# Gated attention and a state-space model, forward and backward: the last key block's transposes moved to TensorE, and the channel stage's constants to the head of the program

## The chip, the cores and the metric

The kernel runs on one core of one Trainium2 chip. The metric is the device time of one execution in microseconds. The time before is 2557.54 us, the median of three runs (2555.94 to 2568.38).

## The reference

The program computes an output and twelve gradients of one layer. The input x is 2048 tokens of 576 features. A gate mixes two branches:

```python
g = _sigmoid((x * gate_w).sum(-1, keepdims=True))
a = _A_ref(x, A_wqkv, A_wo)
b = _B_ref(x, B_A_re, B_A_im, B_B_re, B_B_im, B_C_re, B_C_im, B_log_dt, B_Dskip)
return g * a + (1 - g) * b
```

Branch a is attention with 32 heads of 18 features over all 2048 tokens, followed by the output projection. Branch b is a state-space model: for each of the 576 channels a kernel of length 2048 is made from 128 complex states, and convolved with the channel of x; a skip term is added. The reference returns this output and, by jax.vjp with a given grad_out, the gradients of x, of both attention weights, of the seven parameters of branch b that the convolution uses, of the skip and of the gate.

## The kernel before

The program has a projection stage, an attention stage, a channel stage for branch b, and a closing stage for the last gradients. The change touches the end of the attention stage and the start of the channel stage; this section keeps to those.

**Attention.** The heads are taken in 8 groups of 4, and the queries in 4 blocks of 512. A group with a query block is a unit, so there are 32 units. Each unit goes over 16 key tiles of 128 keys, in 32 steps of a loop whose counter is G; the backward work of a unit runs 39 steps (OFF) behind its forward work. When the forward work has run out, the last unit's backward work still goes on; that is the drain. The order on the engines is written out by hand (a manual schedule), so each engine does its instructions in the order of the code.

For one key tile, TensorE makes scores and dP in PSUM (`ps_P`), ScalarE makes the exponentials `eb` from them, and VectorE makes the products `ds` for four heads (L1488). From `ds` come three things: dV goes by `accV`, dQ by `accQ`, and dK by `accK`. dK needs `ds` turned, keys against queries, in a tile `dsT` that holds two key tiles. A burst of `accK` (`dk_half`) reads one or two of these tiles; there are four key blocks of four tiles, and the last one is tiles 12 to 15.

There are three ways to turn `ds`:

- a DMA transpose that SP issues (L1498), for the first heads of a tile;
- `turn` with `ds_tiles`: the fourth head (index 3), by eight TensorE transposes for a pair of tiles, into a PSUM tile `turn_p` and out again by one copy (L1121); `by_pe` says for how many tiles of a pair;
- `turn_mid`: in the last unit only, the heads 1 and 2 of a tile, by eight TensorE transposes into one of the two PSUM pairs that the scores use (`ps_turn`), and out by one copy (L1143).

So in the last unit head 0 comes by DMA, heads 1 and 2 by `turn_mid` and head 3 by `turn`. When the last unit's gradients are done, `store_grad` (L1086) issues DMA transposes of them on SP, and GpSimd copies these into `dtk` (L1091) and sends them off (L1092).

**The channel stage.** Its channels are taken in 18 blocks of 32. Its first lines (L1526 to L1537) make four constants: `pidx_i` (the partition's number, by GpSimd), `l0col` and `l1col` (the number, and the number plus one, by VectorE), and `sel` (a mask, by GpSimd). Then it opens block 0, in this order: `prep_rx` (VectorE and ScalarE copy x and its gradient to `RX`, L603 to L605; ScalarE's two scale by `l1col` and `l0col`), `load_en`, `wk_cast` (ScalarE, `wk`, L763), `k0` (64 small matmuls of `E1n` with `wk` into the PSUM tile `misc`), `k0_out` (ScalarE copies it to `K0c`, SP sends it to `Kp_d`, L780), `t0_load` (SP loads `T0w` from `Kp_d`, L864), `turn_e` (32 TensorE transposes of `E1n` into `etp`, L672, copied out to `E1e` by VectorE, L673), `m_sum` (eight small matmuls of `skw` with `sel` into `misc`), `m_fin` (ScalarE copies these to `RX` and `dDs_row`, L653 to L655), `m_skw` (SP loads `skw` of block 1, L642) and `uv` (32 matmuls `uvp` from `RX` and `E1e`, copied out by ScalarE, L709). After the opening the blocks follow one another, each with a long scan on VectorE.

Of the kernel before, what the change touches and what calls it, by code (L numbers as in the profile page):

```python
# [9 lines left out]
A = mybir.AluOpType  # L10
ACT = mybir.ActivationFunctionType
BF = mybir.dt.bfloat16
F32 = mybir.dt.float32
# [4 lines left out]
P = 128  # L18


def build(tc, aps, dbg_aps=None, stages=("s1", "attn", "post", "s4", "final")):
    nc = tc.nc
# [20 lines left out]
    NT = S // P  # L43
# [17 lines left out]
    with ExitStack() as gctx:  # L61
# [27 lines left out]
        SUB = 16  # L89
        NSUB = P // SUB  # L90
# [21 lines left out]
        DH2 = D // 2  # L112
        HALF = ((0, DH2), (DH2, D - DH2))
        W3 = 3 * H

        HB = P // 2
        assert D - (DC - 1) * P == HB
# [526 lines left out]
        def m_sum(b):  # L644
            skw = skws.pop(b)
            for v in range(CB // 8):
                mm(dkp(b)[:, v * 8:v * 8 + 8], lhsT=skw[:, v, :], rhs=Q["sel"])
# [113 lines left out]
        def wk_cast(b):  # L761
            wk = blk(b)["wk"] = Q["pw"].tile([P, 2, CB], BF, tag="wk", bufs=2, name="wk")
            nc.scalar.copy(wk, par_of(b)[:, 8:10, :])  # L763
# [187 lines left out]
        if "attn" in stages:  # L951
# [7 lines left out]
            with ExitStack() as ctx:  # L959
# [143 lines left out]
                def s_pair(kind):  # L1103
                    return apsp.tile([P, 2, KB], F32, tag="S", bufs=2, name="ps_" + kind)

                def by_pe(u, p):

                    return 2 if u == units[-1] else {1: 1, NPF: 0, NPF + 1: 1}.get(p, 2)

                def turn(tiles, outs):  # L1110

# [23 lines left out]
                def turn_mid(i):  # L1135

                    U = UN[units[-1]]
                    pt_ = s_pair("turn").rearrange("p a b -> p (a b)").bitcast(BF)[:, 0:2 * KB].rearrange("p (t b) -> p t b", b=P)
                    for x in range(2):
                        for qb in range(TPQ):  # L1140
                            nc.tensor.transpose(pt_[:, x * TPQ + qb, :], U["ds"][i][:, 1 + x, qb * P:(qb + 1) * P], ident_bf)
                    d_ = U["dsT", i // 2][:, i % 2, TPQ:3 * TPQ, :]
                    return lambda: (nc.scalar.copy if now[0] < NTOT + OFF else nc.vector.tensor_copy)(d_, pt_)  # L1143
# [218 lines left out]
                for G in range(NTOT + OFF + 24):  # L1362
# [37 lines left out]
                    if ("f1", G) in todo:  # L1400
                        acc = apsp.tile([P, KB], F32, tag="accO", name="accF")
                        evs.append(todo.pop(("f1", G))[0](acc))
                        e_done[0] += 1.4
                    elif G == NST + 5:
                        evs.append(turn(*do_tile(UN[units[0]])))
                    elif 0 <= m_ < NTOT // 8:
                        u_, kq = divmod(m_, NQ)
                        g, b = units[u_]
                        if slot in SLOTS:
                            nm, burst, h = SLOTS[slot]  # L1410
                            if h == 0:
                                acc = accB("acc" + nm)
                                fill(acc, NFILL[nm])
                                burst(g, b, kq, 0, acc)
                            else:
                                evs.append(burst(g, b, kq, 1, acc))
                                if nm == "Q" and kq == NQ - 1 and u_ < NU - 2:
                                    gq.append((UN[(g, b)], g, b))
                                elif nm == "Q" and kq == NQ - 1:
                                    at(("pre", G + 2), lambda g=g, b=b: store_grad(UN[(g, b)].pop("dqa"), g, (0,), b * TPQ))  # L1420
                                elif nm == "K" and b == NQ - 1:
                                    at(("pre", G + (2 if g == NG - 1 else (11, 13, 17, 17)[kq])), lambda g=g, kq=kq: store_grad(DKV.pop(("v", g, kq)).bitcast(BF), g, (2, 1), kq * TPQ, DKV.pop(("t", g, kq))))
                        else:
                            p = 2 * kq + (slot == 4)
                            t_, o_ = ds_tiles((g, b), p) if by_pe((g, b), p) else ([], [])
                            if p == 1 and gq:
                                t2, o2 = gb_tile()
                                t_, o_ = t2 + t_, o2 + o_
                            if G % NST == 5 and G // NST - 1 < NU:
                                t2, o2 = do_tile(UN[units[G // NST - 1]])  # L1430
                                t_, o_ = t2 + t_, o2 + o_
                            evs.append(turn(t_, o_))
                    if r2:
                        g, b, s2 = r2
                        T = grp_t[g]
# [38 lines left out]
                    for (kind, g, b, i, j, ps) in rows:  # L1474
                        U = UN[(g, b)]
                        if kind == "P1":
                            U["PT"][i, j // 2] = pt_tile()
                            nc.scalar.activation(U["PT"][i, j // 2], ps, ACT.Exp)  # L1478
                        elif kind == "P3":
                            e = eds.tile([P, 2, 448], BF, tag="eb", bufs=8, name="eb").rearrange("p a b -> p (a b)")  # L1480
                            U["eb"][(i[0], i[1], j)] = e[:, 0:KT]
                            U["eb"][(i[0], i[1], j + 2)] = e[:, KT:KW]
                            nc.scalar.activation(e, ps.rearrange("p x q -> p (x q)")[:, KB - KT:2 * KB], ACT.Exp)  # L1483
                        else:
                            if i not in U["ds"]:
                                U["ds"][i] = eds.tile([P, 4, KB], BF, tag="ds", bufs=5, name="ds")
                                U["dsn", i] = 0
                            nc.vector.tensor_tensor(U["ds"][i][:, j, :], ps, U["PT"][i, j // 2][:, j % 2, :], op=A.mult)  # L1488
                            U["dsn", i] += 1
                            while evs:  # L1490
                                evs.pop(0)()
                            nj = 1 if (g, b) == units[-1] else 3 if by_pe((g, b), i // 2) >= 2 - i % 2 else 4
                            if j == nj - 1:
                                p = i // 2
                                assert U["dsn", i] >= nj
                                if i % 2 == 0:
                                    U["dsT", p] = work.tile([P, 2, 4 * TPQ, P], BF, tag="dsT", bufs=3, name="dsT")
                                nc.sync.dma_start_transpose(out=U["dsT", p][:, i % 2, 0:nj * TPQ, :],  # L1498
                                                            in_=U["ds"][i][:, 0:nj, :].rearrange("p j q -> p (j q)"))
                    for e_ in mids + tail + todo.pop(("f2", G), []):  # L1500
                        e_()
                    while packs and packs[0][0] <= G:
# [8 lines left out]
        if "s4" in stages:  # L1511
# [6 lines left out]
            nc.vector.memset(ones_f, 1.0)  # L1518

            with ExitStack() as ctx:  # L1520
                pc = ctx.enter_context(tc.tile_pool(name="s4l", reuse_waits="tile", bufs=1))
                pw = Q["pw"] = Q["en", 2] = ctx.enter_context(tc.tile_pool(name="s4lw", reuse_waits="tile", bufs=1))
                ple_cm = tc.tile_pool(name="s4le", reuse_waits="tile", bufs=1)
                Q["ple"] = ple_cm.__enter__()
                pps = Q["ps"] = ctx.enter_context(tc.tile_pool(name="s4lps", reuse_waits="tile", bufs=1, space=bass.MemoryType.PSUM))
                pidx_i = pc.tile([P, 1], mybir.dt.int32, name="pidx_i")  # L1526
                nc.gpsimd.iota(pidx_i, pattern=[[0, 1]], base=0, channel_multiplier=1)
                l0col = pc.tile([P, 1], F32, name="l0col")
                nc.vector.tensor_copy(l0col, pidx_i)
                l1col = pc.tile([P, 1], F32, name="l1col")  # L1530
                nc.vector.tensor_scalar(l1col, l0col, 1.0, None, op0=A.add)
                sel = pc.tile([P, NSUB], F32, name="sel")
                nc.gpsimd.memset(sel, 1.0)
                nc.gpsimd.affine_select(out=sel, in_=sel, compare_op=A.is_ge, fill=0.0,
                                        base=0, pattern=[[-SUB, NSUB]], channel_multiplier=1)
                nc.gpsimd.affine_select(out=sel, in_=sel, compare_op=A.is_ge, fill=0.0,
                                        base=SUB - 1, pattern=[[SUB, NSUB]], channel_multiplier=-1)  # L1537
                Q["l0col"], Q["l1col"], Q["sel"] = l0col, l1col, sel
                Q["psM"] = lambda: pps.tile([P, 4, P], F32, tag="bk", bufs=4, name="psM")
                misc2 = Q["misc2"] = []  # L1540
# [7 lines left out]
                with tc.manual_schedule(engines={mybir.EngineType.SP}):  # L1548
                    prep_rx(0, dve_copy)
                    load_en(2, 0, nc.sync.dma_start)  # L1550
                    wk_cast(0)
                    k0(0)
                    k0_out(0)
                    t0_load(0)
                    turn_e(0, 0, 0, 4, dve_copy)
                    m_sum(0)
                    m_fin(0)
                    m_skw(1)
                    uv(0, 0)
                    prep_rx(1, dve_copy)  # L1560
# [406 lines left out]
```

## Time and profile before

| | |
|---|---|
| median of three runs | 2557.54 us |
| the profiled execution's own time | 2556.3 us |
| its span (first to last instruction) | 2554.6 us |
| mean granted clock of TensorE | 0.983 |
| busy TensorE, VectorE, ScalarE, GpSimd | 87%, 89%, 88%, 71% |
| the last accV burst of attention starts | 1969.19 us |
| the first uvp of the channel stage starts | 1992.57 us |

The profile is of one execution. PE is TensorE's matmuls, PEld its weight loads, DVE VectorE, ACT ScalarE, POOL GpSimd and SP SyncE, which issues DMAs. A row of the timeline has the start and the length in microseconds, the engine and line, the operation with output and inputs, and in square brackets how long the engine had been idle and what ended that. A row of the waits has the total, the number and the longest. In a table by stage the clock is TensorE's granted clock as a share of full speed.

### The profile page before, as it was taken

To read this page: it belongs to the slowest core of one execution; us is meant where nothing else is said; L and a number is where in the kernel's file an instruction comes from. 1 tells how busy PE (TensorE), PEld (TensorE's weight loads), DVE (VectorE), ACT (ScalarE), POOL (GpSimd) and SP (SyncE) were. 2 spreads that over 40 slices of the span, in tenths; PEclk is the share of its full clock that TensorE was granted. 3 is DMA by queue.
4 is the path that set the end of the run, shared out by engine and by line. 5 is a ranking of instruction groups with operands and counts; after the bars stand their busy time and mean duration, and the time that the engine had idled before them with its cause. 6 is when DMAs were issued, how large, how long until landed. Compare 5 with 4: busy or idle time off the path is not lost.

```text
span 2554.6 us, 72340 instructions
## 1 busy us (share of the span) xinstructions
PE 2232.1 (87%) x28463; PEld 1157.8 (45%) x28463; DVE 2275.6 (89%) x4121; ACT 2256.5 (88%) x2760; POOL 1822.1 (71%) x2829
## 2 busy tenths in 40 slices
PE   8988888888888888888888888888888899999989
PEld 4433333333333333333333333333333799999656
DVE  4849999999999989999999999999996799999964
ACT  5589999999999999999999999999987799998221
POOL 0389988888989888988888988898841255555331
PEclk9989999999999989999999999999999899999999
DMA  7759999999999999998999999999979789987996
GB/s 240 201 125 185 180 188 211 199 187 205 199 194 196 211 184 186 199 209 184 188 208 196 184 200 211 179 191 208 183 158 206 197 257 263 265 258 238 274 252 131
DMA packets 1272236, 519.05 MB, mean 203 GB/s; under 512 B 1187041, under 2 KB 1224530, under 8 KB 1269590
## 3 DMA queue, kind: packets, MB, share of 16 engines
q1 hardware_dynamic: 1223974, 368.17, 75.8%
q0 software_dynamic: 45904, 140.73, 20.5%
q10 hardware_dynamic: 2016, 5.51, 0.7%
q8 instruction: 223, 3.65, 0.6%
q14 instruction: 119, 0.97, 0.1%
HBM read 149.42 MB, written 96.94 MB: 96 GB/s over the span
## 4 chain that ended last, share of the span: by engine, by line
ACT 30%; PE 30%; DVE 21%; issue 4%; DMA 3%; POOL 0%; SPq 0%; DVEq 0%; ACTq 0%; POOLq 0%
ACT PT L1478 15%; ACT eb L1483 13%; PE ps_P L30 12%; DVE ds L1488 7%; PE accV L30 3%; DVE tz L734 3%; DVE wab L754 3%; DVE dvacc L1211 2%; PE accQ L30 2%; PE ps_dx L30 2%; PE accO L30 2%; DVE tz L737 2%; DVE HG L739 2%; DMA dsT<-ds 2%; PE accK L30 1%
## 5 line engine op out<-in xcount | busy, mean ns | idle before, releaser
L1488 DVE TENSOR_TENSOR ds<-ps_P,PT 128x512 bf16<-128x512 f32 x2048 | 1319.8, 683 | 62.7 <-PE ps_P L30 55.7
L1478 ACT ACTIVATE PT<-ps_P 128x1024 bf16<-128x1024 f32 x1024 | 1115.4, 1090 | 13.0 <-PE ps_P L30 11.1
L1483 ACT ACTIVATE eb<-ps_P 128x896 bf16<-128x896 f32 x1024 | 999.1, 976 | 21.3 <-PE ps_P L30 20.9
L30 PE MATMUL ps_P<-dOaT,VaT_g 32*128 32x512 bf16 x2048 | 784.6, 385 | 2.4 <-DVE ds L1488 1.4
L30 PE MATMUL ps_P<-QaT_g,KaT_g 32*128 32x512 bf16 x2048 | 403.2, 384 | 204.5 <-ACT PT L1478 173.6
L507 POOL TENSOR_TENSOR et<-eG,eT 128x448 f32<-128x448 f32 x576 | 542.4, 962 | 10.2
L30 PE MATMUL ps_P<-KaT_g,QaT_g 32*128 32x384 bf16 (+1 forms) x2048 | 401.0, 360 | 4.7 <-ACT eb L1483 0.8
L30 PEld LDWEIGHTS <-KaT_g 32*128 32x128 bf16 x2048 | 162.0, 91 | 492.4 <-issue 468.8
L507 POOL TENSOR_TENSOR Eo<-et,et 128x448 bf16<-128x448 f32 x288 | 327.1, 1136 | 20.3
L30 PEld LDWEIGHTS <-QaT_g 32*128 32x128 bf16 x2048 | 107.2, 91 | 239.0 <-issue 201.8
L30 PE MATMUL accO<-PT,Vtok_g 128*32 128x512 bf16 x2048 | 212.2, 392 | 0.5 <-DVE Ob L1059 0.5
L30 PE MATMUL accV<-eb,dOa 128*32 128x384 bf16 (+1 forms) x2048 | 183.0, 364 | 9.1 <-DVE dsT L1121 8.2
L30 PEld LDWEIGHTS <-VaT_g 32*128 32x128 bf16 x2048 | 184.6, 91 | 3.7 <-issue 2.1
L30 PE MATMUL accQ<-ds,Ktok_g 128*32 128x512 bf16 x2048 | 158.7, 386 | 24.7 <-DVE dvacc L1211 18.7
L30 PE MATMUL accK<-dsT,Qtok_g 128*32 128x256 bf16 x4096 | 159.7, 276 | 14.7 <-DMA dsT<-ds 12.4
L30 PEld LDWEIGHTS <-dOa 128*32 128x32 bf16 x3072 | 78.0, 95 | 122.2 <-issue 88.1
L1121 DVE COPY dsT<-turn_p 128x1024 bf16<-128x1024 bf16 (+1 forms) x216 | 130.5, 604 | 1.0 <-PE turn_p L1115 1.0
L673 ACT COPY E1e<-etp 128x1024 bf16<-128x1024 bf16 x132 | 125.3, 1065 | 3.1 <-PE etp L672 3.1
L1115 PE MATMUL turn_p<-ident_bf,ds 128*128 128x128 bf16 x1552 | 126.0, 221 | 2.1 <-DVE gb L1229 1.4
L30 PEld LDWEIGHTS <-Qtok_g 128*32 128x32 bf16 x4096 | 86.8, 96 | 82.1 <-issue 67.9
L507 POOL TENSOR_TENSOR et<-eT 128x32 f32<-128x32 f32 (+3 forms) x288 | 115.8, 422 | 11.4
L560 POOL DMA_DIRECT2D E_d<-Eo x144 | 84.7, 588 | 42.8 <-POOL Eo L507 42.8
(307 smaller groups left out, 3778.7 us busy)
## 6 DMA issues: line engine op xcount, KB each, us to landing
E_d<-Eo POOLq DMA_DIRECT2D x144, 256.0 KB, 3.8
E1n<-E_d POOLq DMA_DIRECT2D x30, 1024.0 KB, 7.5
T0w<-Kp_d SPq DMA_DIRECT2D x18, 1024.0 KB
xs<-xb_d POOLq DMA_DIRECT2D x28, 512.0 KB, 10.2
dsT<-ds SPq DMA_TRANSPOSE x512
dqkv_d<-dtk POOLq DMA_DIRECT2D x96, 72.0 KB, 4.4
Md_d<-mst SPq DMA_DIRECT2D x18, 288.0 KB
skw<-Md_d SPq DMA_DIRECT2D x72, 64.0 KB
```

Of the source, the lines that this page charges most:

```text
L30: return nc.tensor.matmul(out, lhsT=lhsT, rhs=rhs, start=start, stop=stop, **kw)
L507: nc.gpsimd.tensor_tensor(out, a, b, op=op)
L560: nc.gpsimd.dma_start(E_d[:, q // EQ, 0:EQ * 2 * P], Eo.pop(q).rearrange("p c r n -> p (c r n)"))
L673: copy(E_[:, 4 * q:4 * q + 4], pt_)
L734: nc.vector.tensor_tensor(tz[x], HG[:, :, k - 1].unsqueeze(1).to_broadcast([P, 2, 2, n, CB]), ZZ.unsqueeze(3).to_broadcast([P, 2, 2, n, CB ...
L737: nc.vector.tensor_tensor(tz[x][:, 0], tz[x][:, 0], UVk[:, :, :, k, :], op=A.add)
L754: nc.vector.tensor_tensor(wab, h_, w_, op=A.mult)
L1115: nc.tensor.transpose(pt_[:, x, qb, :], t_[:, qb * P:(qb + 1) * P], ident_bf)
L1121: (nc.scalar.copy if NTOT <= now[0] < NTOT + OFF else nc.vector.tensor_copy)(o_(), src_)
L1478: nc.scalar.activation(U["PT"][i, j // 2], ps, ACT.Exp)
L1483: nc.scalar.activation(e, ps.rearrange("p x q -> p (x q)")[:, KB - KT:2 * KB], ACT.Exp)
L1488: nc.vector.tensor_tensor(U["ds"][i][:, j, :], ps, U["PT"][i, j // 2][:, j % 2, :], op=A.mult)
```

## The change

The change has three parts.

The four constants are made at the head of the program, in the pool `const`, instead of at the start of the channel stage. All the tiles of the attention stage lie 128 bytes higher in SBUF by this; those of the channel stage stay where they were.

In the last unit, all four heads of the tiles 12 to 15 are turned by TensorE: `turn_mid` does sixteen transposes into a whole PSUM pair, and two copies take them out, ScalarE's for the heads 0 and 1 and VectorE's for the heads 2 and 3. In the built program VectorE's copy of a pair waits for ScalarE's. The DMA transposes of these four tiles are gone, and so are the two last rounds of `turn` (sixteen transposes, two copies) of this unit. TensorE's transposes are sixteen more in all.

In the opening of the channel stage `turn_e`, `m_sum` and `m_fin` of block 0 stand ahead of `k0`, `k0_out` and `t0_load`. The first matmul into `misc` for `k0` then comes behind the last copy of `m_fin`.

```diff
@@ setup
+        pidx_i = const.tile([P, 1], mybir.dt.int32, name="pidx_i")
+        nc.gpsimd.iota(pidx_i, pattern=[[0, 1]], base=0, channel_multiplier=1)
+        l0col = const.tile([P, 1], F32, name="l0col")
+        nc.vector.tensor_copy(l0col, pidx_i)
+        l1col = const.tile([P, 1], F32, name="l1col")
+        nc.vector.tensor_scalar(l1col, l0col, 1.0, None, op0=A.add)
+        sel = const.tile([P, NSUB], F32, name="sel")
+        nc.gpsimd.memset(sel, 1.0)
...
@@ by_pe
-                    return 2 if u == units[-1] else {1: 1, NPF: 0, NPF + 1: 1}.get(p, 2)
+                    if u == units[-1]:
+                        return 2 if p < NT // 2 - 2 else 0
+                    return {1: 1, NPF: 0, NPF + 1: 1}.get(p, 2)
@@ turn_mid
+                    if i >= NT - 4:
+                        for x in range(4):
+                            for qb in range(TPQ):
+                                nc.tensor.transpose(pt_[:, x * TPQ + qb, :], U["ds"][i][:, x, qb * P:(qb + 1) * P], ident_bf)
+
+                        def both():
+                            for y, copy in enumerate((nc.scalar.copy, nc.vector.tensor_copy)):
+                                sl = slice(2 * y * TPQ, 2 * (y + 1) * TPQ)
+                                copy(U["dsT", i // 2][:, i % 2, sl, :], pt_[:, sl])
+                        return both
@@ the loop over G
-                            evs.append(turn(t_, o_))
+                            if t_:
+                                evs.append(turn(t_, o_))
...
-                                nc.sync.dma_start_transpose(out=U["dsT", p][:, i % 2, 0:nj * TPQ, :],
-                                                            in_=U["ds"][i][:, 0:nj, :].rearrange("p j q -> p (j q)"))
+                                if (g, b) != units[-1] or i < NT - 4:
+                                    nc.sync.dma_start_transpose(out=U["dsT", p][:, i % 2, 0:nj * TPQ, :],
+                                                                in_=U["ds"][i][:, 0:nj, :].rearrange("p j q -> p (j q)"))
@@ the channel stage
-                pidx_i = pc.tile([P, 1], mybir.dt.int32, name="pidx_i")
-                nc.gpsimd.iota(pidx_i, pattern=[[0, 1]], base=0, channel_multiplier=1)
...
                     wk_cast(0)
+                    turn_e(0, 0, 0, 4, dve_copy)
+                    m_sum(0)
+                    m_fin(0)
                     k0(0)
                     k0_out(0)
                     t0_load(0)
-                    turn_e(0, 0, 0, 4, dve_copy)
-                    m_sum(0)
-                    m_fin(0)
                     m_skw(1)
```

VectorE at the end of the drain, before: from the last products of the tiles to `RX`, with the one copy of `turn_mid`, the one of `turn`, and the constants `l0col` and `l1col`.

```order
L1249 TENSOR_TENSOR dvacc<-dkacc,accK 128x512
L1488 TENSOR_TENSOR ds<-ps_P_38856,PT 128x512
L1488 TENSOR_TENSOR ds<-ps_P_38868,PT 128x512
L1488 TENSOR_TENSOR ds<-ps_P_38882,PT 128x512
L1488 TENSOR_TENSOR ds<-ps_P_38903,PT 128x512
L1488 TENSOR_TENSOR ds<-ps_P_38922,PT 128x512
L1211 TENSOR_TENSOR dvacc<-dvacc,accV 128x512
L1143 COPY dsT<-ps_turn 128x1024
L1229 SCALAR_TENSOR_TENSOR gb<-accQ,dqa 128x512
L1121 COPY dsT<-turn_p 128x2x512
L1518 MEMSET ones_f 128x1
L1529 CAST l0col<-pidx_i 128x1
```

The same place on VectorE in the changed program; `ds` is L1515 there, the pair's copy L1162.

```order
L1162 COPY dsT<-ps_turn 128x1024
L1515 TENSOR_TENSOR ds<-ps_P_38859,PT 128x512
L1275 TENSOR_TENSOR dvacc<-dkacc,accK 128x512
L1515 TENSOR_TENSOR ds<-ps_P_38881,PT 128x512
L1515 TENSOR_TENSOR ds<-ps_P_38893,PT 128x512
L1515 TENSOR_TENSOR ds<-ps_P_38898,PT 128x512
L1162 COPY dsT<-ps_turn 128x1024
L1515 TENSOR_TENSOR ds<-ps_P_38926,PT 128x512
L1515 TENSOR_TENSOR ds<-ps_P_38945,PT 128x512
L1237 TENSOR_TENSOR dvacc<-dvacc,accV 128x512
L1162 COPY dsT<-ps_turn 128x1024
L1255 SCALAR_TENSOR_TENSOR gb<-accQ,dqa 128x512
```

The copies of the tiles 13, 14 and 15 (and 12, above this piece) now stand among the products, and nothing stands behind `gb` but `ones_f` and the addition of `accK`.

ScalarE from the last `eb` of attention to the first `uv`, before:

```order
L1483 ACTIVATE eb<-ps_P_38918 128x896
L604 ACTIVATE RX<-RXn,l1col 128x32x15
L605 ACTIVATE RX<-RXn,l0col 128x32x15
L763 CAST wk<-par 128x64
L779 CAST K0c<-misc_39070 128x32
L653 CAST RX<-misc_39070 128x32
L654 ACTIVATE RX<-misc_39070,l0col 128x32
L655 CAST dDs_row<-misc_39070 1x32
L709 ACTIVATE UV<-uvp 128x64x8 x4
```

And in the changed program, where the copy of a pair is L1162 and the others have the numbers 13 higher:

```order
L1510 ACTIVATE eb<-ps_P_38941 128x896
L1162 COPY dsT<-ps_turn 128x1024
L617 ACTIVATE RX<-RXn,l1col 128x32x15
L618 ACTIVATE RX<-RXn,l0col 128x32x15
L776 CAST wk<-par 128x64
L666 CAST RX<-misc_39079 128x32
L667 ACTIVATE RX<-misc_39079,l0col 128x32
L668 CAST dDs_row<-misc_39079 1x32
L792 CAST K0c<-misc_39079 128x32
L722 ACTIVATE UV<-uvp 128x64x8 x4
```

ScalarE's last copy of attention is now that of tile 15, and `K0c` has moved from before the three copies of `m_fin` to behind them.

More of the change, by code (lines that the diff above doesn't have):

```diff
@@ L114, in build @@
         W3 = 3 * H
+        pidx_i = const.tile([P, 1], mybir.dt.int32, name="pidx_i")
[6 more added lines that the diff above has]
+        nc.gpsimd.memset(sel, 1.0)
+        nc.gpsimd.affine_select(out=sel, in_=sel, compare_op=A.is_ge, fill=0.0,
+                                base=0, pattern=[[-SUB, NSUB]], channel_multiplier=1)
+        nc.gpsimd.affine_select(out=sel, in_=sel, compare_op=A.is_ge, fill=0.0,
+                                base=SUB - 1, pattern=[[SUB, NSUB]], channel_multiplier=-1)
         HB = P // 2
@@ L1137, in turn_mid @@
                     U = UN[units[-1]]
-                    pt_ = s_pair("turn").rearrange("p a b -> p (a b)").bitcast(BF)[:, 0:2 * KB].rearrange("p (t b) -> p t b", b=P)
+                    pt_ = s_pair("turn").rearrange("p a b -> p (a b)").bitcast(BF).rearrange("p (t b) -> p t b", b=P)
+                    if i >= NT - 4:
[7 more added lines that the diff above has]
+                        return both
+                    pt_ = pt_[:, 0:2 * TPQ]
                     for x in range(2):
@@ L1520, in build @@
             with ExitStack() as ctx:
-                pc = ctx.enter_context(tc.tile_pool(name="s4l", reuse_waits="tile", bufs=1))
                 pw = Q["pw"] = Q["en", 2] = ctx.enter_context(tc.tile_pool(name="s4lw", reuse_waits="tile", bufs=1))
@@ L1525, in build @@
                 pps = Q["ps"] = ctx.enter_context(tc.tile_pool(name="s4lps", reuse_waits="tile", bufs=1, space=bass.MemoryType.PSUM))
-                pidx_i = pc.tile([P, 1], mybir.dt.int32, name="pidx_i")
-                nc.gpsimd.iota(pidx_i, pattern=[[0, 1]], base=0, channel_multiplier=1)
[L1528 to L1537, printed above, removed]
                 Q["l0col"], Q["l1col"], Q["sel"] = l0col, l1col, sel
```

## The prediction

> **What bounds the kernel now.** The page first: its span, the busy times of the engines, and the chain that ended last.
>
> ```profile
> span 2554.6 us, 72340 instructions
> PE 2232.1 (87%) x28463; PEld 1157.8 (45%) x28463; DVE 2275.6 (89%) x4121; ACT 2256.5 (88%) x2760; POOL 1822.1 (71%) x2829
> ACT 30%; PE 30%; DVE 21%; issue 4%; DMA 3%; POOL 0%; SPq 0%; DVEq 0%; ACTq 0%; POOLq 0%
> ```
>
> Three engines are near 88% busy and the chain passes among them; nothing the change does to busy time matters here (sixteen transposes more, two copies more). What can matter is a stretch in which all three stand still. The table by stage shows one, at the seam between attention and the channel stage (columns: length, busy PE, PEld, DVE, ACT, POOL, then the granted clock):
>
> ```profile
> 1955.00:1965.00 10.00, 9.26 (x113) 4.08 (x111) 8.67 (x15) 8.41 (x10) 0.84 (x2) 1.00 1.19 240
> 1970.00:1975.00 5.00, 1.80 (x27) 0.97 (x24) 2.33 (x4) 0.00 (x0) 0.00 (x0) 1.00 1.33 227
> 1975.00:1980.00 5.00, 0.95 (x24) 0.59 (x28) 0.06 (x1) 0.00 (x0) 0.00 (x0) 0.71 0.94 281
> 1980.00:1985.00 5.00, 0.87 (x17) 0.40 (x10) 1.69 (x4) 1.22 (x2) 3.28 (x7) 0.50 0.70 194
> 1985.00:1990.00 5.00, 3.89 (x85) 3.89 (x85) 1.15 (x3) 1.24 (x3) 3.46 (x8) 0.50 0.91 249
> ```
>
> From 1970 to 1985 TensorE works 3.6 of 15 us, VectorE 4.1, ScalarE 1.2. The waits around it say for what:
>
> ```profile
> ACT RX L604 <- DVE l1col L1531: 14.6, 1, 14.6
> PE accK L30 <- DMA dsT<-ds: 6.2, 2, 3.8
> PE misc L30 <- ACT wk L763: 5.2, 1, 5.2
> DVE l0col L1529 <- POOL sel L1533: 3.4, 1, 3.4
> ```
>
> TensorE waits twice for a DMA transpose of ds, 6.2 us. Then it waits 5.2 us for ScalarE's wk, which stands behind ScalarE's RX, which waits for l1col, which VectorE can't make before GpSimd's iota, which stands behind a GpSimd copy. The timeline puts these in order. TensorE:
>
> ```profile
> 1969.19 0.40 PE L30 MATMUL accV<-eb,dOa 128*32 128x384 bf16 x4 [0.65 <-ACT eb L1483]
> 1969.53 0.62 PE L1141 MATMUL ps_turn<-ident_bf,ds 128*128 128x128 bf16 x8
> 1972.22 0.61 PE L1115 MATMUL turn_p<-ident_bf,ds 128*128 128x128 bf16 x8 [0.79 <-DVE gb L1229]
> 1976.62 0.64 PE L30 MATMUL accK<-dsT,Qtok_g 128*32 128x256 bf16 x16 [3.80 <-DMA dsT<-ds]
> 1979.69 1.05 PE L30 MATMUL accK<-dsT,Qtok_g 128*32 128x256 bf16 x16 [2.43 <-DMA dsT<-ds]
> 1986.11 1.84 PE L30 MATMUL misc<-wk,E1n 128*128 128x1 bf16 x64 [5.24 <-ACT wk L763]
> 1987.82 3.33 PE L672 MATMUL etp<-ident_bf,E1n 128*128 128x128 bf16 x32
> 1990.98 1.01 PE L30 MATMUL misc<-sel,skw 128*128 128x8 f32 x8
> 1992.57 1.95 PE L30 MATMUL uvp<-RX,E1e 128*128 128x64 bf16 x32 [0.58 <-ACT dDs_row L655]
> ```
>
> The last accV burst of attention starts at 1969.19, accK ends at 1980.74, and uvp, the first real work of the channel stage, starts at 1992.57. So the seam has two pieces: 11.55 us from accV to accK's end, and 11.83 us from there to uvp. From uvp on, blocks follow one another by the three engines, and I found no wait there that ends at a fixed time, so a shift of uvp should reach the end of the program.
>
> **Part 1, the constants at the head.** GpSimd and VectorE at the seam:
>
> ```profile
> 1981.26 0.43 POOL L1091 COPY dtk<-dkacc 128x288 bf16<-128x288 bf16 x1 [14.43 <-DMA dkacc<-dvacc]
> 1983.27 0.15 DVE L1529 CAST l0col<-pidx_i 128x1 f32<-128x1 int32 x1 [3.44 <-POOL sel L1533]
> 1983.78 1.14 ACT L604 ACTIVATE RX<-RXn,l1col 128x480 bf16<-128x480 bf16 x1 [14.63 <-DVE l1col L1531]
> 1984.83 1.10 ACT L605 ACTIVATE RX<-RXn,l0col 128x480 bf16<-128x480 bf16 x1
> 1985.83 0.23 ACT L763 CAST wk<-par 128x64 bf16<-128x64 f32 x1
> ```
>
> With the constants in place, ScalarE runs RX and wk directly behind its last copy of attention, at about 1975 to 1977.4 (1.14 + 1.10 + 0.23), during TensorE's last accK. The wait of 5.2 us for wk goes to nothing. At the head of the program the five GpSimd instructions come in among others that nobody waits for:
>
> ```profile
> 0.80 0.20 POOL L66 MEMSET ident_bf<- 128x128 bf16 x1 [0.29 <-POOLq L1951]
> 5.42 0.69 DVE L232 COPY xT<-tr 128x1024 bf16<-128x1024 bf16 x1 [4.42 <-PE tr L229]
> 40.14 0.68 POOL L429 DMA_DIRECT2D QKV_d<-stg  x1 [36.56 <-ACT qn L408]
> ```
>
> GpSimd idles 36.56 us there and VectorE 4.42 us; cost nothing. If that cover were gone it would be about 1 us (five instructions at the 0.20 of ident_bf's row).
>
> **Part 2, transposes by TensorE alone.** Four DMA transposes leave SP, so the 6.2 us of waits for them end. In exchange each of key tiles 12 to 15 has sixteen transposes and a ScalarE copy with a VectorE copy behind it. What these last, and how far VectorE has room:
>
> ```profile
> 1967.30 1.02 ACT L1143 COPY dsT<-ps_turn 128x1024 bf16<-128x1024 bf16 x1
> 1962.69 0.69 DVE L1488 TENSOR_TENSOR ds<-ps_P,PT 128x512 bf16<-128x512 f32 x1 [0.55 <-PE ps_P L30]
> 1968.24 0.69 DVE L1488 TENSOR_TENSOR ds<-ps_P,PT 128x512 bf16<-128x512 f32 x1 [0.66 <-PE ps_P L30]
> 1970.26 0.69 DVE L1143 COPY dsT<-ps_turn 128x1024 bf16<-128x1024 bf16 x1
> 1971.47 0.69 DVE L1229 SCALAR_TENSOR_TENSOR gb<-accQ,dqa 128x512 bf16<-128x512 f32 x1 [0.53 <-PE accQ L30]
> ```
>
> This is the added wait. In the built program VectorE's copy of a pair waits for ScalarE's of that pair, and the ds products of the next tiles are queued behind it on VectorE; TensorE's ps_P banks, and ScalarE's eb behind them, wait for those. I estimate a hold of 0.75 us for each (1.0 us of copy less what VectorE still has to do of ds) and 0.69 us of copy, for tiles 12 to 14: 4.3 us of VectorE time in a drain that has idle time of 1.6 us there (the 0.55 and 0.66 above are the larger pieces). Propagated by hand, instruction by instruction, with these durations, the last accV comes 3.3 us later; bounds 0 (all in idle time) and 4.3 (none of it).
>
> Behind accV: 0.34 to tile 15's transposes, 1.2 for sixteen (two rows of eight, 0.62), ScalarE's copy 1.0, VectorE's 0.7, gb 0.6, then accK in two bursts of 0.6 (the row with 0.64): 5.0 us, where before it was 11.55 (accQ's sixteen matmuls now lie beside the copies). The first piece gains 11.55 − 5.0 − 3.3 = **3.2 us**, bounds 2.2 and 6.5.
>
> **Part 3, the opening's new order.** E1n's transposes (etp), m_sum and m_fin move ahead of k0. Of these only k0 needs wk, and the first uvp needs all. So from accK's end: etp, m_sum, a wait for m_fin on ScalarE, k0, uvp. The price of 32 etp at the full clock is half of this later row:
>
> ```profile
> 2000.03 3.82 PE L672 MATMUL etp<-ident_bf,E1n 128*128 128x128 bf16 x64
> ```
>
> 1.9 + 1.0 + 0.6 + 1.8 = 5.3 us, instead of 11.83: **6.5 us**. At 0.50, as granted before, etp is 3.3 and the rest alike: 6.7 us, gain 5.1. I take the full clock, because the longest idle of TensorE should now be about 1.5 us (accQ to accK) instead of 3.8, 2.4 and 5.2, and rows at 1970 to 1975 with 1.80 of 5 us busy still show 1.00. VectorE has meanwhile accK's addition, its part of RX (about 1 us, as ScalarE's) and four E1e copies at the 0.69 of its dsT copy: from 1977.6 these end at about 1982.1, uvp starts at 1982.9. That is the next thing to be late, by 0.8 us of room.
>
> [...]
>
> Moved on the queues: Kp_d, T0w and block 1's skw stand behind K0c on SP.
>
> ```profile
> 1988.20 0.32 SPq L780 DMA_DIRECT2D Kp_d<-K0c  x1
> 1993.54 0.32 SPq L864 DMA_DIRECT2D T0w<-Kp_d  x1
> 1993.95 2.54 SPq L642 DMA_DIRECT2D skw<-Md_d  x4
> 2003.69 1.01 PE L30 MATMUL misc<-sel,skw 128*128 128x8 f32 x8
> 2023.49 2.10 PE L30 MATMUL yp<-RX,T0w 128*128 128x32 bf16 x32
> ```
>
> K0c came 4.4 us before uvp and now comes with it, so these start some 4.8 us later against the rest. T0w has 30 us until yp; cost nothing. skw was issued until 1996.5 and used at 2003.69; it would be issued until about 1991.5 and be used at 1994.0. [...] I take 0; bound 2.
>
> **The sum.** 3.2 + 6.5 = 9.7 us. The profiled execution took 2556.3 us, 1.7 beyond its span, and becomes 2546.6; the median of three, 2557.54, lies 1.2 higher and would be 2547.8. I say **2547.2**. Bounds: 2.2 + 5.1 − 2 = 5.3 and 6.5 + 6.5 = 13.0.
>
> **Rivals.** The forecast: chance 0.61 for a gain of 5 to 12.
>
> A, the drain isn't stretched: VectorE's held copies fit into its idle time. The gain is 13.0, 2543.9; for it speaks that VectorE idles 1.6 us there, that one ScalarE copy (turn_p, 1.0 us) is gone, and that SP is freed; against it, VectorE at 8.67 of 10 us. [...] Chance of over 12.8: 0.13.
>
> B, VectorE's hold cascades: each late ds makes eb late and each late eb the next copy, twice the 4.3 us. The first piece then loses 2.1, and 6.5 − 2.1 leaves 4.4: 2552.5. Decided if the last accV comes more than 6.5 us later. Chance 0.13.
>
> C, the constants weren't the last thing that RX waited for: its memory comes free only with the DMA of dkacc, for which GpSimd at 1981.26 had waited 14.43 us. That DMA comes 3.3 later with the drain, so RX starts at 1984.6, wk is done at 1987.1, m_fin behind it at 1987.7, k0 at 1989.5, and uvp gains 3.1: 2553.8. For it: GpSimd's row. Against: in the new order RX waits only for ds, accQ and eb. It decides if RX starts after 1978.0, 2.5 us ahead of the end of m_sum. Chance 0.08.
>
> D, slower: the transposes take one of the two PSUM pairs that the scores also use, and keep it until VectorE's copy is through. If that copy comes behind all four ds products of a tile, the pair is held for 1.2 of transposes, 2.8 of ds (four of 0.69), 1.0 of ScalarE's copy and 0.7 of its own, 5.7 us, and if the next scores wait all that time, tiles 12 to 14 cost 17 us against the 13.0 that can be gained at most: 2561. It decides from 4.3 us a tile on. For it: two pairs alone; against: the scores have the other one, and ScalarE has no more copies than before. Chance 0.05, of which 0.02 over 0.5%.
>
> **The numbers.** A measurement of this kernel can tell about 0.5%, 12.8 us. Faster by more than that: A, 0.13. Slower: 0.02. Same: 0.85, with the forecast, B, C and most of D in it. The range leaves out about 2 in 10: from A's time less 2 us for the spread of the runs before, 2541.9, to C's 2553.8 and 1.7 more, 2555.5.
>
> **What would show it.** Right: accK without a DMA wait and its end near 1977.6; RX on ScalarE by 1976; etp directly behind accK at a clock near 1.00; uvp near 1982.9; later rows 9 to 10 us earlier. Wrong: a wait on ScalarE's RX for anything later than 1976; VectorE waits of over 2 us for ScalarE's dsT copies; uvp waiting for E1e; m_sum of block 1 waiting for skw; or later blocks that aren't earlier by what uvp is.

## The result and the profile after

The changed kernel takes 2592.15 us (2587.29 to 2600.18, six runs) where the kernel before takes 2557.47 in the same job: a ratio of 1.0128, with a 95% interval of 1.0111 to 1.0144. Forecast were 2547.2 us and no more than 2555.5. So the change costs 33 us by this ratio (35 by the medians) where 10 were to be gained.

The seam is not where they went. TensorE's rows there, in the changed kernel (they answer to those from 1969.19 to 1992.57 of before):

```profile
2013.95 0.62 PE L30 MATMUL accV<-eb,dOa 128*32 128x384 bf16 x4 [0.36 <-ACT eb L1510]
2014.50 1.89 PE L1157 MATMUL ps_turn<-ident_bf,ds 128*128 128x128 bf16 x16
2018.86 1.06 PE L30 MATMUL accK<-dsT,Qtok_g 128*32 128x256 bf16 x32 [0.80 <-DVE ones_f L1546]
2019.85 1.96 PE L685 MATMUL etp<-ident_bf,E1n 128*128 128x128 bf16 x32
2021.65 1.01 PE L30 MATMUL misc<-sel,skw 128*128 128x8 f32 x8
2023.24 0.17 PE L30 MATMUL misc<-dsk_row,ident_bf 1*128 1x32 bf16 x1 [0.58 <-ACT dDs_row L668]
2023.35 1.78 PE L30 MATMUL misc<-wk,E1n 128*128 128x1 bf16 x64
2024.99 3.38 PE L30 MATMUL uvp<-RX,E1e 128*128 128x64 bf16 x32
```

accK's two waits for a DMA are gone, and so is the wait for wk. (accV works on eb, as its row shows, and not on ds as the section on the kernel has it.) From accV to accK's end it is 5.97 us (forecast 5.0, before 11.55), from there to uvp 5.07 (forecast 5.3, before 11.83). But all of this lies some 40 us late. VectorE copies oT once in each of the 32 forward units, so the start of this copy in each unit shows when the delay came about. Before, units 1, 5, 6 and 32:

```profile
167.12 0.68 DVE L1047 COPY oT<-accO 128x512 f32<-128x512 f32 x1
387.56 0.68 DVE L1047 COPY oT<-accO 128x512 f32<-128x512 f32 x1
443.09 0.68 DVE L1047 COPY oT<-accO 128x512 f32<-128x512 f32 x1
1897.60 0.68 DVE L1047 COPY oT<-accO 128x512 f32<-128x512 f32 x1
```

The same four in the changed kernel:

```profile
169.81 0.68 DVE L1060 COPY oT<-accO 128x512 f32<-128x512 f32 x1
390.42 0.68 DVE L1060 COPY oT<-accO 128x512 f32<-128x512 f32 x1
452.00 0.68 DVE L1060 COPY oT<-accO 128x512 f32<-128x512 f32 x1
1937.48 0.68 DVE L1060 COPY oT<-accO 128x512 f32<-128x512 f32 x1
```

The delay is 2.7 us at unit 1, 2.9 at unit 5, 8.9 at unit 6 and 39.9 at unit 32. It grows in steps of 2.8 to 8.4 us at the units 6, 10, 14, 18, 22, 26 and 30, each the second of a group of heads (and by 2.3 at unit 7), and little or nothing in the units between, where at times a part is won back. None of the change's instructions stands there. What the engines wait for in unit 6 is seen on TensorE, VectorE and ScalarE:

```profile
427.90 1.04 PE L30 MATMUL accK<-dsT,Qtok_g 128*32 128x256 bf16 x16 [4.52 <-DMA dsT<-ds]
429.00 0.69 DVE L1269 COPY dkacc<-accK 128x512 f32<-128x512 f32 x1 [4.79 <-PE accK L30]
429.52 0.92 ACT L1510 ACTIVATE eb<-ps_P 128x896 bf16<-128x896 f32 x1 [4.86 <-PE ps_P L30]
```

A DMA transpose of ds lands 4.5 us too late for accK, and everything stands behind it. The waits of the whole attention stage (us 160 to 1895) and the hardware DMA queue in us 200 to 1900 (packets, MB, time that the packets took as a share of 16 engines), before:

```profile
PE accK L30 <- DMA dsT<-ds: 6.2, 6, 1.3
q1 hardware_dynamic: 1073798, 273.62, 91.8%
```

and in the changed kernel:

```profile
PE accK L30 <- DMA dsT<-ds: 31.8, 18, 4.5
q1 hardware_dynamic: 1052659, 268.32, 97.4%
```

accK's waits for dsT are 25.6 us longer there, where the delay grows by 37.2 (39.9 − 2.7); the rest was not traced. There are fewer packets in the window, as the program is slower, but they take more of the queue's time: 0.918 × 16 × 1700 us / 1073798 = 23.3 ns for one before, and by the same working 25.2 ns now. The queue carries the same transfers in the same order; what differs about them is where their tiles lie: 128 bytes higher, as the section on the change says.

### The profile page after: what moved, and what is told of

Read it like the earlier page. It is cut to its first block, busy times and chain, and to the rows that moved or that the text cites. A ratio compares the mean times of both kernels' runs of the same rounds, so it can differ in the third digit from the quotient of the medians.

```text
span 2585.6 us, 72360 instructions
## 1 busy us (share of the span) xinstructions
PE 2257.6 (87%) x28479; PEld 1163.5 (45%) x28479; DVE 2279.4 (88%) x4123; ACT 2260.4 (87%) x2760; POOL 1825.6 (71%) x2829
## 5 line engine op out<-in xcount | busy, mean ns | idle before, releaser
L1515 DVE TENSOR_TENSOR ds<-ps_P,PT 128x512 bf16<-128x512 f32 x2048 | 1321.1, 684 | 66.5 <-PE ps_P L30 57.1
L30 PE MATMUL ps_P<-QaT_g,KaT_g 32*128 32x512 bf16 x2048 | 408.4, 388 | 197.5 <-ACT PT L1505 168.3
```

The costliest lines, as they stand in the source:

```text
L30: return nc.tensor.matmul(out, lhsT=lhsT, rhs=rhs, start=start, stop=stop, **kw)
```

## The experiments

In the expectations below, e1 is the first kernel, e2 the second, and so on. What is said of a single place in a kernel is read from one profiled execution.

**The place alone, and the change without it.** Theory P: the 128 bytes cost the time. Theory H: something else in the change does, at the head or by way of the queues. The first kernel is the kernel before with nothing but a pad:

```diff
+        eds.tile([P, 32], F32, name="pad")
         d_aT = [eds.tile([P, 4, 512], BF, tag="ds", bufs=5, name="ds") for _ in range(DC)]
```

> The kernel before with nothing changed but an unused pad of 128 bytes ahead of attention's first tile, so that every attention tile lies where the changed kernel has it, and the channel stage's where they were. Theory P (place): the new addresses make the packets of the DMA queue longer, 25.2 instead of 23.3 ns each, and that alone costs the 39 us: 2557.5 + 39 = 2596, between 2588 and 2600, with the accK waits for dsT near 32 us. Theory H (the instructions at the head, or the drain's new transposes, through the queues): addresses don't matter, 2557.5 within 3.

Measured: ratio 1.0207 to before (1.0183 to 1.0231), 2615.16 us. That is more than the changed kernel, which has the seam's gain against it, and 15 us above the range forecast. The accK waits are 31.5 us, as forecast, and the packets take 25.2 ns:

```profile
q1 hardware_dynamic: 1040820, 265.55, 96.3%
```

The pad alone makes the kernel slower than the whole change does. The second kernel is the changed one with more padding at the same place:

```diff
+        eds.tile([P, 96], F32, name="pad")
         d_aT = [eds.tile([P, 4, 512], BF, tag="ds", bufs=5, name="ds") for _ in range(DC)]
```

> The changed kernel with a pad of 384 bytes ahead of attention's first tile: its tiles lie 512 bytes above those of before instead of 128. Theory P, if what counts repeats every 512 bytes or less: attention as before, and the seam's gain is left, some 7 to 8 us: 2549 to 2551. Theory H: 2590 as the changed kernel.

Measured: ratio 0.9973 (0.9961 to 0.9985), 2553.64 us where the kernel before takes 2560.99 in the same job. The gain of 7.4 us is as forecast, the time itself is above the range. In the third, the lines that make the constants stand at the channel stage again:

```diff
-        pidx_i = const.tile([P, 1], mybir.dt.int32, name="pidx_i")
...
+                pidx_i = pc.tile([P, 1], mybir.dt.int32, name="pidx_i")
```

> The changed kernel with the four constants made at the channel stage again, so that attention's tiles lie where they lay before; the transposes by TensorE and the new order of the opening stay. Theory P: no 39 us, and of the seam's gain what the wait for l1col leaves: drain 1 us, and RX at about the place it had, so that wk still comes late but etp and m_sum are done meanwhile: 4 to 6 us faster, 2551 to 2554. Theory H by the head: the same. Theory H by the drain's transposes: 2590.

Measured: ratio 0.9977 (0.9962 to 0.9993), 2556.62 us: 4.4 less than before, where 4 to 6 were forecast; the time itself is again above the range. The fourth has a pad of 128 bytes in the changed kernel:

```diff
+        eds.tile([P, 32], F32, name="pad")
         d_aT = [eds.tile([P, 4, 512], BF, tag="ds", bufs=5, name="ds") for _ in range(DC)]
```

> The changed kernel with a pad of 128 bytes: attention's tiles lie 256 bytes above those of before. Theory P with a period of 256 bytes (ds on a multiple of 256 again): 2549 to 2551. Theory P with a period of 512: anything from 2550 to 2600, since dsT then starts at another place in its 512 bytes. Theory H: 2590.

Measured: ratio 0.9964 (0.9949 to 0.9979), 2551.37 us, 9.6 less than before. The packets take 23.2 ns:

```profile
q1 hardware_dynamic: 1072879, 273.48, 91.6%
```

Theory H is out: with the same instructions and 256 or 512 bytes instead of 128, the change is a gain of about 0.3 to 0.4%. The third and the fourth also price the early constants at the seam: from accK's end to uvp it is 7.94 us in the third and 5.04 in the fourth, 2.9 less.

**Which tile.** ds starts on a multiple of 256 in the kernel before; dsT starts 96 above one. The fifth kernel moves ds by 128 and the rest by 256, the sixth moves all but ds by 128, both from the kernel before:

```diff
+        eds.tile([P, 32], F32, name="pad")
         d_aT = [eds.tile([P, 4, 512], BF, tag="ds", bufs=5, name="ds") for _ in range(DC)]
+        eds.tile([P, 32], F32, name="pad2")
         eb_t = [eds.tile([P, 2, 448], BF, tag="eb", bufs=8, name="eb") for _ in range(DC + 3)]
```

(the sixth without the first of the two pads)

> The kernel before with two unused pads of 128 bytes, one ahead of the ds tiles and one behind them: ds alone starts 128 bytes off a multiple of 256, and the rest of attention lies 256 bytes higher, where e4 showed no loss. Theory S (the source: the DMA transposes read ds in pieces that now cross a boundary at each multiple of 256): as slow as e1, 2595 to 2620, packets at 25 ns. Theory D (the destinations, dsT and PTt, or another tile): as before, 2555 to 2562, packets at 23.3 ns.

> The kernel before with one pad of 128 bytes behind the ds tiles: ds stays, everything else in attention lies 128 bytes higher. Theory S: 2555 to 2562. Theory D: 2595 to 2620. If both matter, both e5 and e6 are slower than before, by less than e1.

Measured: ratio 1.0184 (1.0155 to 1.0213), 2604.85 us, with ds moved, and 1.0027 (1.0006 to 1.0049), 2566.13 us, with the rest moved; the kernel before takes 2559.24 in this job. The fifth lies in theory S's range, the sixth 4 us above it. The queues' lines, the fifth first:

```profile
q1 hardware_dynamic: 1048196, 267.20, 96.3%
```

```profile
q1 hardware_dynamic: 1073732, 273.60, 91.6%
```

25.0 ns a packet against 23.2. It is the place of ds, the source of the transposes. What the rest adds is at most half a per cent, and not by the packets.

The eighth kernel asks for another distance, a pad of 64 bytes in the kernel before (`[P, 16]` instead of `[P, 32]`):

> The kernel before with a pad of 64 bytes ahead of attention's first tile. Theory S: any place off a multiple of 256 makes the 256-byte reads cross, so as slow as e1, 2595 to 2620. If instead 64 bytes cost less than 128 (2560 to 2590), the price goes by how a piece is cut, not by whether.

Measured: ratio 1.0186 (1.0152 to 1.0220), 2604.55 us, 25.1 ns, in the range of theory S. 64 bytes cost as 128 do.

**The destinations, and a second source.** In the seventh, on top of the fourth, the tile ahead of dOaT is 160 bytes longer, which brings dOaT, PTt, dsT, dvacc and gb to multiples of 256; the ninth brings 24 of the 41 PT buffers there too, which are sources of the PTt transposes.

```diff
-                        st["oT"] = work.tile([P, KB], F32, tag="oT", bufs=1, name="oT")
+                        st["oT"] = work.tile([P, KB + 40], F32, tag="oT", bufs=1, name="oT")[:, 0:KB]
...
-                        gT = work.tile([P, TPQ, 4, HP], BF, tag="gT", bufs=1, name="gT")
+                        gT = work.tile([P, KB + 32], BF, tag="gT", bufs=1, name="gT")[:, 0:KB].rearrange("p (t a b) -> p t a b", a=4, b=HP)
```

(the last two lines in the ninth alone)

> The changed kernel as in e4 (256 bytes up), and 160 bytes more ahead of dOaT, so that the destinations dsT and PTt and the sources dvacc and gb start on multiples of 256 instead of 96 above one. Theory S: the packets stay at 22.9 ns, 2551 within 3 (dvacc's few transposes alone may gain a little). Theory D: packets under 22.5 ns and faster than e4.

> As e7, with 64 bytes more behind attention's last work tile, so that 24 of the 41 PT buffers start on multiples of 256 instead of 192 above one. PT is the source of the 128 PTt transposes. Theory S holds for every source: packets about 0.2 ns shorter than e7's 23.20, and up to 4 us faster than e7's 2545. If the queue has room now, the packets shorten and the time stays.

Measured: ratio 0.9951 (0.9925 to 0.9977), 2545.24 us, for the seventh, and 0.9961 (0.9938 to 0.9984), 2549.88 us, for the ninth; both have packets at 23.2 ns, as the fourth has (the forecast for the seventh had it at 22.9). The intervals overlap, so neither the destinations nor PT can be told from nothing. The seventh came out 3 us below theory S's range, and for PT the forecast of 0.2 ns shorter packets failed. The seventh has the lowest median of all; it is faster than the kernel before, but not by this shown faster than the fourth.

**The price of one transpose.** A kernel that leaves the whole computation out and writes zeros issues batches of twelve DMA transposes, with nothing beside them.

```diff
+        for nm, n, so, do in CASES:
+            for y in range(NDST):
+                t = w.tile([P, 2048 + 128], BF, tag=f"d{y}", bufs=1, name=f"dst_{nm}")
+                v = t[:, do:do + n].rearrange("p (t q) -> p t q", q=P)
+                nc.sync.dma_start_transpose(out=v, in_=by[so][:, so:so + n])
```

> Nothing of the computation is left but zeros in the outputs: batches of twelve DMA transposes from SBUF to SBUF alone on the queue, each batch from one source at a set distance from a multiple of 256 bytes to destinations at a set distance. Rows of 4096 bytes (as ds of four heads): source 0 to 0; 128 to 0; 0 to 96; 128 to 96; 64 to 0; 32 to 0; rows of 2048 bytes (as PT): 0, 32, 128; rows of 1024: 0, 128. Theory S: a source off a multiple of 256 takes about 8% longer (25.2 for 23.3 ns a packet) at all three distances and all lengths, and the destination's place changes nothing. Theory S': the source's place costs only beside the other traffic of the kernel, and all batches of one length are alike here. Theory D: the batch 0 to 96 is slower than 0 to 0.

SP's rows, one batch each, with the time from the first issue to the last. (VectorE's reads of the destinations, each behind a landing, keep the same pace: for dst_a 11 steps from us 30.29 to 52.75, 2.04 us each.) Rows of 4096 bytes, source and destination at: 0 and 0 (dst_a), 128 and 0, 0 and 96, 128 and 96, 64 and 0, 32 and 0; rows of 2048 bytes with the source at 0, 32, 128; then dst_a's case again (dst_z):

```profile
26.13 24.30 SPq L45 DMA_TRANSPOSE dst_a<-src  x12
50.53 29.42 SPq L45 DMA_TRANSPOSE dst_b<-src  x12
80.04 24.99 SPq L45 DMA_TRANSPOSE dst_c<-src  x12
105.56 29.51 SPq L45 DMA_TRANSPOSE dst_d<-src  x12
135.16 29.82 SPq L45 DMA_TRANSPOSE dst_e<-src  x12
165.07 29.54 SPq L45 DMA_TRANSPOSE dst_f<-src  x12
194.71 16.35 SPq L45 DMA_TRANSPOSE dst_g<-src  x12
211.15 16.42 SPq L45 DMA_TRANSPOSE dst_h<-src  x12
227.66 16.76 SPq L45 DMA_TRANSPOSE dst_i<-src  x12
275.92 23.81 SPq L45 DMA_TRANSPOSE dst_z<-src  x12
```

With the source on a multiple of 256 one transpose follows another each 2.0 us (24.30 / 12), with the source 32, 64 or 128 off it each 2.45 to 2.49: 21 to 23% more, at any of the three distances. The destination costs some 3% (24.99 against 24.30), little more than the spread of the first case, which gave 24.00 in a batch ahead of these and 23.81 in the last.

That is theory S for these rows, and more than its 8%. That not all packets of the kernel are those of ds explains a part. The rise in the kernel is 1.9 ns over all packets of the queue; about three quarters of them are of ds (an estimate: 487 transposes in the window, by the code three heads in twelve of sixteen and four in the others, 256 bytes a packet, where the queue's mean is 273.62 MB / 1073798 = 254.8), which makes 2.5 ns for one of ds, 11% of 23.3. In the batches the pace is slower by 21 to 23%. Why it is less in the kernel stays open.

With shorter rows theory S does not show in the pace. Rows of 2048 bytes are issued one each 1.36 us, and 0, 32 and 128 are nearly alike; with rows of 1024 bytes both places take 15.61 us for twelve. What sets the pace there was not shown. The medians from issue to landing still differ for 2048 bytes (for 1024 they are 2.3 and 2.4):

```profile
dst_g<-src SPq DMA_TRANSPOSE x12, 2.8
dst_h<-src SPq DMA_TRANSPOSE x12, 3.3
dst_i<-src SPq DMA_TRANSPOSE x12, 3.3
```

So a source with rows as those of PT lands 0.5 us later off the boundary; that this costs anything in the kernel the ninth didn't show.

**The steps at the seam.** The tenth kernel issues the copies of a pair in the other order, on top of the fourth:

```diff
-                            for y, copy in enumerate((nc.scalar.copy, nc.vector.tensor_copy)):
+                            for y, copy in ((1, nc.vector.tensor_copy), (0, nc.scalar.copy)):
```

> The changed kernel as in e4, with the two copies of a pair issued in the other order: VectorE's first, ScalarE's behind it. My step: VectorE is held 0.75 us for ScalarE's copy at each of tiles 12 to 14. Then the hold goes, and the last accV comes 2.0 to 2.3 us earlier than e4's 75.9 us behind the last oT: 73.6 to 73.9. Rival: what stretches the drain is VectorE's own copies and ScalarE's, whichever is first: 75 to 77.

In the fourth kernel, VectorE's copies of the tiles 12 to 14 wait 0.71, 1.32 and 2.16 us for ScalarE's:

```profile
1965.27 0.69 DVE L1163 COPY dsT<-ps_turn 128x1024 bf16<-128x1024 bf16 x1 [0.71 <-ACT dsT L1163]
1969.94 0.69 DVE L1163 COPY dsT<-ps_turn 128x1024 bf16<-128x1024 bf16 x1 [1.32 <-ACT dsT L1163]
1975.78 0.69 DVE L1163 COPY dsT<-ps_turn 128x1024 bf16<-128x1024 bf16 x1 [2.16 <-ACT dsT L1163]
```

In the tenth, ScalarE's wait for VectorE's instead:

```profile
1960.53 1.01 ACT L1163 COPY dsT<-ps_turn 128x1024 bf16<-128x1024 bf16 x1 [1.01 <-DVE dsT L1163]
1965.92 1.01 ACT L1163 COPY dsT<-ps_turn 128x1024 bf16<-128x1024 bf16 x1 [1.45 <-DVE dsT L1163]
1970.49 1.01 ACT L1163 COPY dsT<-ps_turn 128x1024 bf16<-128x1024 bf16 x1 [1.25 <-DVE dsT L1163]
```

Measured, in one execution: the last accV 75.1 us behind oT instead of 75.9, where I had 73.6 to 73.9. My step failed: the wait changes sides, and the time is in the rival's range. The 0.8 us can't be read as a gain, since kernels with the drain of the fourth spread as widely: 74.6 in the second, 74.4 in the seventh, 75.9 in the ninth. What sets these apart, as far as the rows show, is TensorE's clock. The sixteen transposes of tile 14, in the fourth kernel and in the seventh:

```profile
1972.81 1.89 PE L1158 MATMUL ps_turn<-ident_bf,ds 128*128 128x128 bf16 x16
1964.66 1.07 PE L1158 MATMUL ps_turn<-ident_bf,ds 128*128 128x128 bf16 x16
```

The clock was 0.77 in the fourth (us 1970 to 1975); 1.07 us is what sixteen also take in the changed kernel at 2003.28, where the clock is 1.00 (us 2000 to 2005). VectorE's third wait is 2.16 us in the fourth and 1.31 in the seventh. In the tenth too one tile's sixteen were slow: 1.77 us, at 1963.39. Behind accV the tenth gains 0.6 us more (4.24 to accK's end; the second, fourth, seventh and ninth kernel have 4.88).

The eleventh takes the transposes by TensorE out of the fourth:

```diff
-                    if u == units[-1]:
-                        return 2 if p < NT // 2 - 2 else 0
-                    return {1: 1, NPF: 0, NPF + 1: 1}.get(p, 2)
+                    return 2 if u == units[-1] else {1: 1, NPF: 0, NPF + 1: 1}.get(p, 2)
```

(with turn_mid and the DMA transposes as before the change)

> The changed kernel as in e4, with the last key block turned by DMA as before: constants at the head and the new order of the opening alone. My step: the drain is 71.6 us again from oT to accV, accK 11.55 behind it, uvp 5.1 to 5.3 behind that, so the transposes by TensorE are worth 2.4 us and the rest 6.8. Rival: with RX early, ScalarE and VectorE give the DMA's wait another cover and accK's end comes before 11.0.

Measured, in one execution: 71.7 us from oT to accV and 11.3 behind it, close to the forecast and not the rival's, and then 6.65 to uvp instead of 5.1 to 5.3. Its etp, and the table by stage of us 1980 to 1985 (the clock is 0.50):

```profile
1982.83 3.57 PE L686 MATMUL etp<-ident_bf,E1n 128*128 128x128 bf16 x32
```

```profile
1980.00:1985.00 5.00, 3.15 (x37) 2.63 (x38) 2.11 (x4) 2.29 (x3) 1.30 (x2) 0.50 1.05 313
```

While TensorE waits for the DMA, the clock falls (0.94 in us 1975 to 1980, then 0.50), and etp takes 3.57 us. In the fourth kernel it takes 1.96, at a clock of 1.00, though the clock had fallen to 0.77 in the drain ahead of it:

```profile
1982.66 1.96 PE L686 MATMUL etp<-ident_bf,E1n 128*128 128x128 bf16 x32
```

```profile
1970.00:1975.00 5.00, 3.43 (x25) 1.90 (x24) 3.62 (x6) 2.10 (x3) 0.49 (x1) 0.77 1.10 238
1980.00:1985.00 5.00, 3.56 (x77) 3.12 (x69) 3.52 (x7) 2.59 (x4) 1.87 (x3) 1.00 1.03 181
```

So the transposes are worth 3.8 us (89.6 us from oT to uvp here, 85.8 in the fourth), of which 1.6 come by the clock, and the rest of the change 5.4 (95.0 before); forecast were 2.4 and 6.8. Against the second and the seventh, whose sixteen transposes took 1.07 us at each tile, they are worth 5.0 and 5.3.

The eleventh also answers Part 1. There ScalarE was to run RX directly behind its last copy of attention once the constants were early. With early constants alone it does not:

```profile
1981.93 0.06 DVE L1534 MEMSET ones_f<- 128x1 bf16 x1 [5.95 <-DMA dsT<-ds]
1981.99 1.12 ACT L618 ACTIVATE RX<-RXn,l1col 128x480 bf16<-128x480 bf16 x1 [10.41 <-DVE ones_f L1534]
```

RX starts only when the last DMA transpose of ds has landed. In the fourth, without those transposes, it starts 2.5 us behind the last accV and waits for nothing. So the early constants free RX only together with Part 2.

## Why the prediction was wrong

**The step that failed** is Part 1's "cost nothing" for the constants at the head of the program. I priced the instructions there (five on GpSimd by my count; its rows have four) and looked for who waits for them. I didn't price the 128 bytes that they take below attention's tiles, though the shift was known. By the fifth and the first kernel that is worth 1.8 to 2.1% by itself. The claim that "nothing the change does to busy time matters here" and the search for the stretch in which all engines stand still led past it: the DMA queue, whose packets took 91.8% of the time of 16 engines in us 200 to 1900, wasn't among the views that I read for a bound. (This share isn't one of a maximum: over the whole run of the lone batches it is 102.4%, so packets overlap.)

How it comes to 40 us: a transpose of four heads rises by 0.43 us in the lone batches (most of the kernel's have three). In most units the delay doesn't grow, so the queue has the room for this there, as I read it. Where a group of heads begins, SP also issues the new group's loads and the old one's dkacc transposes; there the longer packets make dsT late, by up to 4.5 us at accK in one wait, and TensorE, VectorE and ScalarE stop together. SP's rows ahead of that wait in the changed kernel:

```profile
409.84 1.60 SPq L1099 DMA_TRANSPOSE dkacc<-dvacc  x1
411.54 3.71 SPq L1526 DMA_TRANSPOSE dsT<-ds  x1
415.34 1.26 SPq L1032 DMA_TRANSPOSE Ktok_g<-QKV_d  x1
416.70 2.93 SPq L1526 DMA_TRANSPOSE dsT<-ds  x1
```

That it is these extra transfers which make the difference between the units is read from their place, and wasn't tried by itself.

Why a source off a multiple of 256 bytes costs more was not shown: that the reads then cross a boundary was my guess, by which theory S was made. What the runs show is that the distance makes no difference: 32, 64 and 128 cost the same in the batches (29.54, 29.82 and 29.42 us for twelve), and 64 and 128 in the kernel (25.1 and 25.2 ns a packet).

**The parts that held.** From the last oT to uvp it was 95.0 us before; the fourth kernel, where ds lies well, takes 85.8. That is a gain of 9.2 at the seam where the forecast had 9.7. Term by term:

| | forecast | fourth kernel | second, seventh, ninth |
|---|---|---|---|
| last accV later | 3.3 (0 to 4.3) | 4.3 | 3.0, 2.8, 4.3 |
| accV to accK's end | 5.0 | 4.9 | 4.9 each |
| accK's end to uvp | 5.3 | 5.0 | 5.0 each |
| the sum, less the 23.4 of before | −9.7 | −9.2 | −10.4, −10.7, −9.1 |

The hold on VectorE was mis-sized: 0.71, 1.32 and 2.16 us in the fourth kernel, not 0.75 each. The second is longer, as I read it, because a late ds makes the next pair late as well. The third has 0.85 us of the fallen clock in it: it is 1.31 in the second and the seventh. So B is out: accV came 2.8 to 4.3 us later in these kernels and 4.9 in the changed one (76.5 instead of 71.6 behind oT), over my bound of 4.3 but under the 6.5 that would decide for B. That the sum is so near is in part luck, as the same drain spreads over 1.5 us.

The clock was 1.00 for etp in the fourth kernel, as I took it: us 1980 to 1985, where etp is over half of TensorE's work (1.96 of 3.56 us), has 1.00. In the drain it fell. It was 1.00 there before (us 1950 to 1975); with sixteen transposes a tile, the sixteen of one or two tiles took 1.77 to 1.89 us in five of seven profiled executions (1.89 in the fourth, at the 0.77 above, and in the ninth), and in the second and the seventh each tile's took 1.07. In the changed kernel the clock was 0.50 in us 2010 to 2015; its last sixteen transposes took 1.89 us, and accV to accK's end 5.97. No run tells whether the transposes or the waits around them do this.

skw, which I put at 0, did come late, which the prediction has as a sign of being wrong. In the fourth kernel m_sum waits for it 0.31 and 0.28 us in block 1, and in block 2:

```profile
2011.86 2.26 PE L30 MATMUL misc<-sel,skw 128*128 128x8 f32 x8 [6.18 <-DMA skw<-Md_d]
```

In the changed kernel it waits 2.27 us in block 2. Neither shows in the time: block 3's first uvp is 5.0 us earlier than before (2040.96 for 2045.92), and from the first uvp to the end it is 561.8 us, before 562.0. Other kernels have 560.6 to 566.9 there, so a loss of 2 us, my bound, couldn't be seen. That bound was my estimate and no run shows it.

Of the rivals, A is out, since the drain is stretched. The two copies of a pair never ran side by side, so no run shows what that would cost. C is out for the changed kernel, where RX waits 0.73 us for VectorE's copy of dsT and for no DMA; the eleventh shows a wait of its kind. D ended on the right side, but for a reason that had no part in it.

In the changed kernel itself the sum is: 39.9 late at the last oT, 7.5 won from there to uvp (87.5 instead of 95.0) and 1.4 won behind it: 31.0, the difference of the spans. The first 2.7 of the 39.9 were there at unit 1; the kernels with good places lie there between 1.0 us earlier and 5.5 later than before, so I don't read anything into them.

**What stays open.** The changed kernel and the first kernel have the same addresses in attention and the same price of a packet, but were 39.9 and 56.6 us late at the last oT. In the first kernel more units per group were hit. A part may be the spread of executions: the one profiled is the fastest of six for the changed kernel and the second slowest of four for the first. No run tells what decides the rest.

## What to carry to other kernels

A tile that is added or taken away can move those above it, so here an edit of four small constants was also an edit of the source address of most DMA transposes; look up the addresses before and after, and keep the sources of DMA transposes with long rows on multiples of 256 bytes with a pad that can be named (rows of 4096 bytes here: 2.0 us each, and 2.45 to 2.49 off the multiple). Look at the DMA queue as at a fifth engine: here 8% more time for each packet (25.2 ns for 23.3) came out as waits at a few places, not evenly. And when a delay is found, find where it grew (one row per unit is enough) before looking at the lines that were edited.

## What the runs showed of the hardware

DMA transposes of 128 rows of 4096 bytes within SBUF, alone on the queue, followed one another each 2.0 us with the source on a multiple of 256 bytes and each 2.45 to 2.49 with it 32, 64 or 128 above one; the destination 96 above one changed some 3%, where the same case repeats within some 2%. Twelve with rows of 1024 bytes took 15.61 us in both places. Sixteen TensorE transposes of 128x128 in bf16 took 1.07 us at a granted clock of 1.00 and 1.89 where it had fallen (0.77 over those 5 us); thirty-two took 1.96 at 1.00 and 3.57 at 0.50. Two copies out of one PSUM pair by two engines were one behind the other in this program, in whichever order they were issued: VectorE waited 0.71 to 2.16 us for ScalarE's in the fourth kernel, ScalarE 1.01 to 1.45 for VectorE's in the tenth.
